# Round 0 of an RWKV-6 + MLP kernel: two tiles transposed from padded copies instead of turned by products, masks built together, and a new order of work

## The chip, the core and the metric

One core of one Trainium2 chip. The engines are PE (TensorE: matmuls and weight loads), DVE (VectorE), ACT (ScalarE), POOL (GpSimd), and SP, whose queue issues nearly all DMAs. The metric is the device time of one execution in microseconds (us), lower is better.

## What is computed

A linear-attention block with a decayed state (RWKV-6), and behind it a normalised two-layer MLP with a residual. Everything is float32.

```python
B, H, S, D = 4, 8, 768, 48            # r, k, v, w: (B, H, S, D); u: (H, D)
state = np.zeros((B, H, D, D))
for t in range(S):
    cur = einsum('bhd,bhe->bhde', u[None] * k[t], v[t])
    y[t] = einsum('bhd,bhde->bhe', r[t], state + cur)
    state = w[t][..., None] * state + einsum('bhd,bhe->bhde', k[t], v[t])
x = y.transpose(0, 2, 1, 3).reshape(B, S, 384)
xn = (x - mean) / sqrt(var + 1e-6) * g_ln
out = x + relu(xn @ w_ch1) @ w_ch2    # w_ch1: (384, 1536), w_ch2: (1536, 384)
```

## The kernel before, in words

**Rounds and tiles.** The work is cut into 8 rounds (4 batches, two halves of 384 steps). A round has 3 tiles of 128 steps, and a tile is two groups of 64 rows. For the attention part, r, k and w are loaded as nat_r, nat_k and nat_w (192 KB a tile; in a row lie 2 heads x 4 steps x 48 values). They are turned so that the head dimension lies on the partitions: two heads of a pair stand at partitions 0 to 47 and 64 to 111. Between them is a gap of 16, so a source whose heads are padded from 48 to 64 values can be turned in one piece.

**Round 0 differs from the others.** It has two parts: tile 0 alone, and tiles 1 and 2 together (`parts_of_round`, line 513), so that tile 0 can run ahead. Its r, k and w are turned by `by_head` (line 746): two products with the identity for each row group and step, straight from the unpadded loads. `turn` (751) does this for k and r of one tile into kr_ps (PE), and two copies out of PSUM ("keep") bring it to kr. `whole_row` (827) does it for w into one of the "a" tiles, and a copy brings it to low. The other rounds work on padded tiles pad_k and pad_r, which DVE, POOL and ACT write (`inner`, 596), and `turn` transposes these with one PE.transpose for each row group and step.

**Behind the turning** there is a ladder of 6 levels for each part: `quads` (952) does products of k and r on PE into an "a" tile; `keep` (1008) copies them, masked by that level's mask, into A on DVE; `grow` (984) multiplies kr by the products of w of that level (DVE); `totals` (921) makes the next level's products of w (low, then tot; DVE or POOL). Level l+1 of quads needs level l of grow. `own_terms` (855) does r times u (ru) and the products with k (own), masked by the diagonal. Then come `turn_k`, `states`, `outputs`, the normalisation, and the MLP's `first_product` and second product.

**Masks.** Five level masks, the diagonal and a row-group mask (own) are built by POOL at the start: `build_mask` (470) does, for each level, a memset, two affine selects on a 128 x 64 byte strip of "wide" and two copies of 64 x 32 bytes to mask0..mask4. `build_own_mask` (487) is needed from round 1 on only.

**Weights.** The MLP's weights come as 24 raw loads of 384 KB into 4 buffers, and each is converted by some three instructions of ACT, DVE or POOL (`convert`); a buffer is free when its conversions are done.

**What sets the order.** Every job is announced with `plan.add` (engines with costs, keys read and written) and gets a number in that order. `Plan.ORDER` (74) is a list written out by hand: job number, plus 10000 or 20000 where the second or third allowed engine does it. Each engine works its jobs strictly in that order. `Plan.order` (223) walks the list once; it also places "idle" matmuls on zeros wherever by its own costs PE would wait over 0.35 us (line 2011). A job on POOL that is marked as sharing the port first waits for the DVE jobs listed just before it. Neither the conversions nor rounds 1 to 7 are touched by the change other than through the order.

The heads of the queues, as they follow from the list before:

- PE: k, r of tile 0; w of tile 0; quads level 0 of tile 0; own of tile 0; k, r of tile 2; quads 1 of tile 0; k, r of tile 1; w of tile 2; quads 0 of tiles 1+2; w of tile 1; quads 2 of tile 0; own of tiles 1+2; quads 3, 4, 5 of tile 0; quads 1 of tiles 1+2.
- DVE: A zeroed; second copy of kr tile 0; r times u; keep 0; totals 0; grow 0; own terms; a conversion; grow 1; totals; keep 1; keep 0 of tiles 1+2; ...
- POOL: masks 3, 0, diagonal, masks 2, 4, 1, totals 1, r times u of tiles 1+2, totals, own mask.
- SP: r, w of tile 0, k of tile 2, u_t twice, r 2, k 1, r 1, raw2, w 1, w 2, g, raw4, raw1, v, u_bc, raw0, raw5, w of round 1, raw3, vx.

Of the kernel before, what the change touches and what calls it, by code (L numbers as in the profile page):

```python
# [62 lines left out]
class Plan:  # L63
# [11 lines left out]
        15, 4, 3, 19, 20, 12, 8, 14, 2, 250, 11, 10, 16, 13, 9, 252, 249, 251, 17, 10021, 28, 31, 33, 29, 95,  # L75
        260, 247, 18, 262, 22, 32, 34, 30, 10096, 35, 257, 97, 261, 259, 258, 10023, 24, 25, 36, 248, 255, 256,
        98, 10269, 272, 253, 274, 0, 254, 263, 107, 91, 93, 92, 94, 59, 5, 87, 37, 38, 88, 109, 89, 90, 270,
        111, 433, 103, 60, 39, 439, 10264, 10026, 271, 40, 265, 42, 41, 273, 43, 44, 46, 110, 108, 7, 10266, 45,
        51, 50, 99, 47, 55, 275, 276, 105, 113, 10027, 127, 49, 48, 52, 53, 10054, 61, 100, 106, 129, 6, 277,
        56, 112, 10101, 62, 65, 66, 63, 123, 434, 436, 1, 440, 441, 435, 114, 104, 278, 10064, 102, 279, 115,  # L80
        119, 438, 10267, 139, 69, 67, 57, 70, 58, 68, 71, 128, 130, 373, 280, 281, 282, 72, 444, 73, 125, 74,
        75, 283, 126, 375, 76, 120, 77, 124, 284, 285, 287, 78, 131, 79, 121, 122, 141, 437, 10080, 443, 81, 85,
        83, 288, 142, 286, 303, 10268, 10134, 10084, 82, 86, 293, 301, 10289, 10294, 442, 116, 295, 296, 193,
        305, 304, 143, 300, 292, 297, 298, 291, 290, 10445, 10118, 10117, 306, 309, 225, 227, 223, 302, 446,
        299, 194, 307, 308, 310, 132, 449, 133, 377, 228, 312, 311, 313, 314, 224, 144, 315, 135, 316, 237, 140,
        136, 238, 226, 137, 229, 230, 10450, 239, 235, 233, 10317, 10318, 319, 320, 321, 322, 323, 324, 325,
        447, 240, 138, 10326, 181, 236, 234, 327, 329, 331, 195, 451, 231, 448, 328, 332, 145, 458, 10330, 151,
        10452, 10453, 232, 183, 196, 182, 335, 184, 388, 345, 346, 336, 455, 457, 454, 456, 169, 153, 459, 163,
        627, 337, 338, 374, 185, 460, 461, 152, 462, 469, 389, 10146, 10154, 376, 197, 147, 349, 463, 333, 474,
        473, 475, 350, 465, 392, 464, 378, 149, 466, 341, 468, 467, 393, 155, 156, 148, 482, 150, 476, 347, 403,  # L90
        198, 624, 157, 159, 164, 170, 348, 158, 379, 470, 355, 404, 483, 485, 477, 167, 173, 186, 480, 621, 626,
        187, 625, 342, 334, 161, 339, 241, 245, 486, 10471, 10472, 407, 171, 382, 160, 10380, 10162, 390, 172,
        242, 479, 478, 351, 246, 481, 487, 484, 488, 165, 188, 391, 628, 629, 622, 623, 632, 489, 385, 340, 166,
        352, 175, 177, 176, 179, 191, 490, 343, 243, 353, 491, 178, 10168, 217, 418, 244, 634, 189, 356, 631,
        635, 180, 174, 496, 405, 493, 354, 219, 367, 357, 344, 633, 190, 494, 492, 500, 505, 502, 501, 495, 220,
        506, 394, 630, 192, 637, 406, 368, 638, 636, 497, 211, 381, 213, 499, 218, 10386, 507, 199, 498, 200,
        643, 203, 221, 408, 358, 508, 205, 10639, 10640, 513, 509, 644, 514, 10222, 510, 400, 201, 214, 212,
        202, 420, 215, 204, 645, 10216, 664, 663, 662, 206, 397, 515, 516, 207, 422, 503, 409, 209, 412, 208,
        210, 395, 641, 421, 642, 398, 504, 511, 512, 387, 812, 399, 362, 396, 363, 10401, 661, 402, 520, 364,
        646, 815, 365, 366, 415, 647, 657, 10658, 517, 518, 383, 659, 384, 648, 521, 809, 10416, 10410, 10413,  # L100
        359, 411, 813, 560, 650, 649, 10522, 10519, 523, 524, 525, 526, 654, 419, 360, 655, 527, 528, 529,
        10530, 656, 531, 532, 533, 541, 361, 542, 534, 543, 537, 538, 535, 423, 539, 424, 369, 651, 652, 430,
        653, 816, 665, 570, 417, 814, 565, 370, 667, 544, 536, 668, 540, 666, 670, 10431, 10660, 571, 561, 566,
        811, 810, 545, 671, 555, 414, 572, 427, 428, 562, 573, 425, 371, 563, 10819, 669, 672, 673, 546, 674,
        567, 574, 568, 547, 564, 432, 817, 556, 548, 426, 429, 550, 580, 575, 676, 551, 10821, 569, 549, 557,
        552, 558, 675, 820, 823, 822, 576, 818, 677, 585, 577, 586, 553, 554, 587, 559, 679, 581, 588, 600, 590,
        733, 589, 582, 601, 602, 578, 579, 753, 595, 825, 826, 678, 684, 680, 691, 827, 583, 831, 685, 603, 584,
        687, 686, 596, 695, 696, 697, 688, 10828, 833, 10830, 10824, 698, 832, 829, 682, 693, 604, 597, 694,
        591, 598, 683, 689, 699, 599, 690, 681, 700, 605, 1000, 743, 849, 1003, 850, 997, 692, 836, 701, 705,
        592, 838, 837, 842, 702, 971, 1002, 703, 593, 606, 704, 594, 706, 844, 839, 841, 843, 708, 10707, 607,  # L110
        834, 608, 748, 851, 1005, 1001, 999, 998, 1004, 852, 11007, 709, 10710, 711, 713, 712, 714, 715, 1009,
        716, 717, 835, 720, 10719, 10718, 840, 609, 610, 845, 1008, 721, 1010, 722, 729, 725, 846, 858, 726,
        11006, 730, 723, 727, 724, 728, 731, 1013, 732, 615, 611, 616, 758, 853, 738, 855, 883, 854, 1011, 856,
        612, 744, 734, 11014, 859, 10847, 11012, 1019, 857, 861, 1015, 745, 735, 736, 737, 617, 11016, 863, 862,
        746, 749, 864, 747, 750, 613, 754, 618, 751, 755, 752, 1018, 860, 1021, 1017, 1020, 614, 865, 866, 867,
        1024, 1090, 1087, 1037, 1093, 884, 768, 773, 848, 1040, 1039, 778, 756, 1026, 1025, 871, 769, 619, 868,
        1038, 739, 757, 770, 876, 870, 877, 878, 740, 771, 873, 772, 874, 1094, 788, 1088, 872, 875, 869, 741,
        1027, 889, 783, 890, 1029, 742, 1028, 885, 1091, 886, 1030, 1032, 1031, 784, 759, 1022, 1089, 789, 785,
        786, 760, 887, 790, 1023, 879, 888, 1092, 1041, 1095, 761, 774, 762, 1098, 1096, 1097, 1101, 791, 779,
        775, 880, 776, 780, 777, 936, 1042, 1043, 372, 763, 781, 793, 1100, 792, 764, 782, 881, 891, 765, 892,  # L120
        11099, 1045, 1044, 1103, 1104, 1109, 1110, 1046, 893, 894, 1105, 11106, 11107, 1111, 11108, 766, 794,
        767, 895, 787, 882, 896, 795, 798, 897, 10898, 899, 1047, 1049, 1114, 1102, 11033, 901, 900, 902, 903,
# [212 lines left out]
def kernel(  # L335
# [12 lines left out]
    nc = tc.nc  # L348
# [121 lines left out]
    def build_mask(lev):  # L470
# [8 lines left out]
        for i in range(2):  # L479
            rows = ds(C * i, C)  # L480
            POOL.tensor_copy(out=masks[lev][rows], in_=wide[lev][rows, ds(C // 2 * i, C // 2)])
# [1571 lines left out]
```

## Time and profile before

| what | value |
|---|---|
| median of 3 runs | 499.63 us (496.48 to 505.93) |
| the profiled execution, its own time | 494.83 us |
| its span, first to last instruction | 492.8 us |
| mean granted TensorE clock | 0.996 |
| PE busy | 479.1 us (97%), 26.55 us of it "idle" filler matmuls |
| DVE, ACT, POOL busy | 351.2, 256.6, 114.6 us |
| DMA | 57.39 MB, mean 116 GB/s |

How to read it: nearly all instructions bear line 46, that of the wrapper through which the kernel issues them, so one goes by tile names. "kr_ps<-ident,nat_r" is a product of k or r, "a<-ident,nat_w" one of w, "a<-kr" a quad, "kr_ps<-ident,pad_r" a transpose of the later rounds, "mask<-wide" a copy of a finished mask. In a timeline row stand start, length, engine, operation, output<-input, shape and count, and in brackets what the engine waited for before it. "issue" is time in which the engine waited for nothing that the profile shows. A span on POOL is rough.

### The profile page before, as it was taken

Reading aid. Unit: us, or ns where it says so; the run is one execution under the profiler, and the core shown is the slowest. Engines: PE = TensorE matmul, PEld = TensorE weight load, DVE = VectorE, ACT = ScalarE, POOL = GpSimd, SP = SyncE. Lnnn points to the kernel's source line nnn. Section 1 sums busy time; section 2 is a strip of 40 time slices with the busy share of each in tenths; the row PEclk is TensorE's granted clock in tenths of the full one; section 3 lists DMA queues with packets and bytes.
Section 4 is the critical chain, followed back from the end, with each engine's and each line's share of the span. In section 5 each row is a group of like instructions: output and inputs, shape, how many; then the busy total and the mean of one; then the engine's idle time right before and its main releaser. Section 6 shows DMA issues by size and latency. Waiting matters only on the chain.

```text
span 492.8 us, 18752 instructions
## 1 busy us (share of the span) xinstructions
PE 479.1 (97%) x8215; PEld 406.6 (83%) x8215; DVE 351.2 (71%) x694; ACT 256.6 (52%) x585; POOL 114.6 (23%) x127
## 2 busy tenths in 40 slices
PE   8799999999999999999999999998999999999996
PEld 6667887667986779966888776788999999999996
DVE  6689899997975994877684796978667355345334
ACT  3569988964485217625635517476643243232231
POOL 8433404441311510131820660002300000000000
PEclk9989999999999999999999999999999999999999
DMA  7677388248946327347338605230331221223301
GB/s 205 181 216 189 106 193 241 61 121 210 255 99 175 57 66 180 98 121 165 122 102 198 188 4 100 67 76 5 96 98 50 76 86 43 85 64 93 117 0 48
DMA packets 102113, 57.39 MB, mean 116 GB/s; under 512 B 58256, under 2 KB 98704, under 8 KB 102032
## 3 DMA queue, kind: packets, MB, share of 16 engines
q1 hardware_dynamic: 101760, 56.01, 43.3%
q8 instruction: 64, 1.05, 0.9%
q10 hardware_dynamic: 272, 0.20, 0.1%
q14 instruction: 17, 0.14, 0.1%
HBM read 45.81 MB, written 8.01 MB: 109 GB/s over the span
## 4 chain that ended last, share of the span: by engine, by line
PE 85%; ACT 6%; DVE 3%; issue 2%; POOL 2%; DMA 1%; SPq 0%; DVEq 0%; POOLq 0%; ACTq 0%
PE h_ps L46 30%; PE a L46 25%; PE o L46 16%; PE o_2P L46 3%; PE kr_ps L46 3%; PE idle L46 3%; PE o_2D L46 2%; PE xT_ps L46 2%; PE kn_ps L46 1%; ACT rest L46 1%; DMA d<-w1d 1%; POOL tot L46 1%; ACT rx L46 1%; ACT held L46 1%; DVE x L46 1%
## 5 line engine op out<-in xcount | busy, mean ns | idle before, releaser
L46 PE MATMUL o<-ffn,h 128*128 128x384 f32 x288 | 101.6, 495 | 0.0
L46 ACT ACTIVATE h_ps<-h_ps 128x384 f32<-128x384 f32 x84 | 39.5, 475 | 71.8 <-PE h_ps L46 66.7
L46 PEld LDWEIGHTS o<-ffn,h 128*128 128x128 f32 x288 | 52.1, 189 | 29.4
L46 DVE TENSOR_TENSOR kr<-kr,tot 112x1536 f32<-112x1536 f32 (+2 forms) x36 | 60.2, 1673 | 13.3 <-PE a L46 13.1
L46 DVE SCALAR_TENSOR_TENSOR hL<-h_ps,hH 128x384 fp32r<-128x384 f32 x48 | 26.5, 555 | 57.9 <-ACT hH L46 57.3
L46 PEld LDWEIGHTS a<-kr 48*60 48x60 f32 (+5 forms) x3264 | 42.8, 122 | 10.1 <-issue 5.3
L46 PE MATMUL h_ps<-xd,d 128*128 128x384 f32 x204 | 49.3, 350 | 0.4 <-DMA d<-w1d 0.4
L46 PE MATMUL a<-kr 48*60 48x32 f32 (+5 forms) x3264 | 47.2, 209 | 1.3 <-issue 0.8
L46 PE MATMUL h_ps<-xhl,wl 128*128 128x384 f32 x180 | 44.5, 354 | 1.2 <-issue 1.2
L46 ACT ACTIVATE hH<-h_ps 128x384 fp32r<-128x384 f32 x48 | 23.2, 491 | 41.0 <-PE h_ps L46 40.9
L46 PE MATMUL h_ps<-xhl,wh 128*128 128x384 f32 x180 | 41.4, 338 | 0.0
L46 PEld LDWEIGHTS h_ps<-xd,d 128*128 128x128 f32 x204 | 35.7, 188 | 2.1 <-issue 0.5
L46 ACT COPY kr<-kr_ps 112x512 f32<-112x512 f32 x47 | 26.2, 587 | 20.5 <-PE kr_ps L46 20.3
L46 ACT ACTIVATE h<-h_ps 128x384 f32<-128x384 f32 (+2 forms) x60 | 24.9, 425 | 20.5 <-PE h_ps L46 20.0
L46 PEld LDWEIGHTS h_ps<-xhl,wl 128*128 128x128 f32 x180 | 31.5, 188 | 3.5 <-issue 1.5
L46 PE MATMUL a<-xkr,hH 128*128 128x384 f32 x96 | 32.4, 337 | 0.0
L46 PEld LDWEIGHTS h_ps<-xhl,wh 128*128 128x128 f32 x180 | 32.4, 188 | 0.0
L46 DVE COPY_PREDICATED A<-mask,a 128x768 f32<-128x768 int8 (+2 forms) x31 | 28.2, 910 | 4.4 <-PE a L46 4.2
L46 PE MATMUL idle<-nought 128*128 128x128 f32 (+2 forms) x86 | 26.6, 417 | 1.0 <-DVE eps L46 1.0
L46 DVE SCALAR_TENSOR_TENSOR hD<-hH,hL 128x384 fp32r<-128x384 f32 x48 | 26.2, 555 | 0.9
L46 PE MATMUL h_ps<-xf,w 128*128 128x128 f32 (+1 forms) x144 | 25.9, 332 | 0.0
L46 PE MATMUL a<-sx,rx 48*64 48x48 f32 x384 | 23.7, 218 | 1.8 <-issue 1.3
(195 smaller groups left out, 1098.0 us busy)
## 6 DMA issues: line engine op xcount, KB each, us to landing
d<-w1d SPq DMA_DIRECT2D x84, 192.0 KB, 3.0
raw<-in_moe_w_ch_dram SPq DMA_DIRECT2D x24, 384.0 KB, 4.0
nat_r<-in_r_dram SPq DMA_DIRECT2D x24, 192.0 KB, 3.8
nat_w<-in_w_dram SPq DMA_DIRECT2D x24, 192.0 KB, 4.1
v<-in_v_dram SPq DMA_DIRECT2D x24, 192.0 KB, 4.5
nat_k<-in_k_dram SPq DMA_DIRECT2D x23, 192.0 KB, 3.8
w1d<-w1diff SPq DMA_DIRECT2D x12, 192.0 KB, 3.6
out_dram<-x SPq DMA_DIRECT2D x4, 576.0 KB, 3.7
```

The lines of the kernel that those rows point to most:

```text
L46: ins = self.tc.keep_in_program_order(f(*args, **kw))
```

## The change

Three things. (1) Tiles 1 and 2 of round 0 are no longer turned by `by_head`: two copies pad k and r into the tiles pad_k and pad_r, a third pads w into a borrowed "x" tile (pad_w, its gap zeroed by a memset), each on any of ACT, DVE and POOL, and PE transposes them as in the other rounds. Tile 0 stays as it was. (2) The masks of levels 1 to 4 become one job behind mask 0's: one memset for all five strips, the ten selects as before, and two copies for four levels together. (3) The order list is new in its whole length, and the plan's instruction counts for the products are doubled.

```diff
-    masks = {lev: const.tile([P, C // 2], I8, name=f"mask{lev}") for lev in range(NLEV - 1)}
+    masks = const.tile([P, NLEV - 1, C // 2], I8, name="masks")
...
-    def build_mask(lev):
-        n = 1 << lev
-        m = wide[lev].rearrange("p (q n) -> p q n", n=n)
-        POOL.memset(m, 1.0)
-        for base, sign in ((0, 1), (n - 1, -1)):
-            POOL.affine_select(
-                out=m, in_=m, compare_op=ALU.is_ge, fill=0.0, base=base,
-                pattern=[[-2 * n * sign, C // n], [0, n]], channel_multiplier=sign,
-            )
+    def build_masks(levels):
+        if 0 in levels:
+            POOL.memset(wide, 1.0)
+        for lev in levels:
+            n = 1 << lev
+            m = wide[:, lev].rearrange("p (q n) -> p q n", n=n)
+            for base, sign in ((0, 1), (n - 1, -1)):
+                POOL.affine_select(
+                    out=m, in_=m, compare_op=ALU.is_ge, fill=0.0, base=base,
+                    pattern=[[-2 * n * sign, C // n], [0, n]], channel_multiplier=sign,
+                )
+        some = slice(levels[0], levels[-1] + 1)
         for i in range(2):
             rows = ds(C * i, C)
-            POOL.tensor_copy(out=masks[lev][rows], in_=wide[lev][rows, ds(C // 2 * i, C // 2)])
+            POOL.tensor_copy(out=masks[rows, some], in_=wide[rows, some, ds(C // 2 * i, C // 2)])
...
+    def unpadded(part):
+        return part[0] == part[1] == 0
...
-                        if rnd == 0:
+                        if unpadded(part):
                             by_head(to[:, n, s], f"nat_{nm}0", c, s, rows)
                             continue
                         PE.transpose(
...
     def whole_row(part):
         rnd, c0, nc = part
+        n = nc * Q * 2 * D
+        w_pad = f"pad_w{c0}"
+
+        def roomy():
+            t = tile_("x", w_pad, [P, TT, H, D]).rearrange("p c h d -> p (c h d)")
+            return t[:, 0 : nc * Q * 2 * HP].rearrange("p (s c j d) -> p s c j d", s=Q, c=nc, j=2)
+
+        def copy(e, nm):
+            src = natural(nm, part).rearrange("p s b d -> p b s d")
+            if nm == "w":
+                to = roomy().rearrange("p s c j d -> p (c j) s d")[..., 0:D]
+            else:
+                to = padded(nm, part).rearrange("p s b d -> p b s d")
+            (ACT.copy if e == "ACT" else BY[e].tensor_copy)(out=to, in_=src)
+
+        if not unpadded(part):
+            plan.add("POOL", 0.35, lambda: POOL.memset(roomy()[..., D:], 0.0), ...)
+            for nm in "wkr":
+                plan.add(("ACT", "DVE", "POOL"), ..., lambda e, nm=nm: copy(e, nm), ...)
...
                 for s in range(Q):
                     for i in range(2):
-                        by_head(t[:, i, s], "nat_w0", c, s, ds(C * i, C))
+                        rows = ds(C * i, C)
+                        if unpadded(part):
+                            by_head(t[:, i, s], "nat_w0", c, s, rows)
+                            continue
+                        PE.transpose(
+                            t[:, i, s], roomy()[rows, s, c - c0].rearrange("p j d -> p (j d)")[:, 0:PD],
+                            ident[rows, rows],
+                        )
...
-            for lev in range(NLEV - 1):
+            for levels, cost_ in (((0,), 1.7), (range(1, NLEV - 1), 3.5)):
                 plan.add(
-                    "POOL", 1.5, lambda lev=lev: build_mask(lev), r=["wide"], w=[("mask", lev)],
-                    pri=lev - 40, port=False,
+                    "POOL", cost_, lambda levels=levels: build_masks(levels), r=["wide"] + [("mask", 0)] * (0 not in levels),
+                    w=[("mask", lev) for lev in levels], pri=levels[0] - 40, port=False,
                 )
...
     ORDER = [
-        15, 4, 3, 19, 20, 12, 8, 14, 2, 250, 11, 10, 16, 13, 9, 252, 249, 251, 17, 10021, 28, 31, 33, 29, 95,
+        2, 14, 9, 7, 8, 12, 10015, 10019, 20, 4, 3, 16, 17, 248, 10, 11, 247, 249, 10018, 25, 28, 26, 246, 13,
+        250, 10252, 30, 29, 253, 258, 261, 262, 259, 263, 245, 0, 244, 10260, 21, 104, 31, 27, 1, 20251, 256,
```

Three mask jobs fall away and four jobs come (250 the memset, 251, 252 and 253 the copies of w, k and r), so the later jobs' numbers are moved. The heads of the queues after:

- PE: w of tile 0; k, r of tile 0; quads 0 of tile 0; own of tile 0; k, r of tile 1; k, r of tile 2; quads 1 of tile 0; w of tile 2; w of tile 1; quads 0 of tiles 1+2; quads 2 of tile 0; own of tiles 1+2; quads 3, 4, 5 of tile 0; quads 1 of tiles 1+2.
- DVE: A zeroed; copy of low tile 0; totals 1 of tile 0; second copy of kr tile 0; r times u; **copy k**; keep 0; grow 0; a copy of kr tile 1; totals; own terms; keep 1; r times u of tiles 1+2; totals; grow 1; keep 0 of tiles 1+2; keep 2; grow 2; a sign conversion; own terms of tiles 1+2; keep 3; grow 3; grow 0 of tiles 1+2; grow 4; ...
- POOL: own mask; diagonal; mask 0; totals 0 of tile 0; masks 1 to 4; memset of pad_w; g_top; **copy w**; totals 0 of tiles 1+2; ...
- ACT: first copy of kr tile 0; **copy r**; three copies of kr tiles 2, 1; two copies of low; conversions.
- SP: w, r of tile 0, r 1, u_t twice, k 2, r 2, k 1, w 2, g, w 1, raw4, raw5, r of round 1, raw0, raw1, w of round 1, raw2, v, raw3, raw10, raw8, vx.

## The prediction

> **What bounds the kernel now.** I read the page first, then busy time by stage, then the chain of waits up to 60 us, then the timelines of PE, DVE and POOL up to 27 us.
>
> The page and the busy time by stage (columns: stretch, its length, busy time and instructions of each engine, granted clock, DMA share, GB/s):
>
> ```profile
> span 492.8 us, 18752 instructions
> ```
> ```profile
> 5.00:17.00 12.00, 8.92 (x375) 7.36 (x365) 5.94 (x12) 4.72 (x9) 8.59 (x22) 1.00 0.87 245
> 17.00:25.00 8.00, 7.49 (x238) 5.67 (x230) 7.07 (x11) 5.00 (x11) 3.07 (x8) 1.00 0.56 145
> 25.00:37.00 12.00, 11.25 (x329) 8.57 (x328) 10.08 (x21) 8.57 (x24) 3.62 (x6) 0.86 0.77 220
> 37.00:50.00 13.00, 12.87 (x332) 10.19 (x329) 12.96 (x35) 12.47 (x32) 4.03 (x5) 1.00 0.67 179
> ...
> 62.00:75.00 13.00, 13.00 (x265) 10.73 (x265) 12.66 (x24) 10.89 (x24) 1.72 (x1) 1.00 0.82 197
> ```
>
> From 62 us on PE is full. Before that it only looks full: of PE's 26.55 us of filler ("idle") matmuls, 22.1 lie before 50 us and 0.9 between 50 and 62. So up to 25 us round 0 runs on a chain of single steps (DVE is busy for 13.0 of the 20 us from 5 on, ACT for 9.7); from 37 to 50 us DVE (12.96 of 13 us) and ACT (12.47) are the bound; from then on it is PE. Everything that the change names lies in the first stretch. What it gains there reaches the end only as an earlier start of the same later work.
>
> The chain of waits (start, length, what) and PE's timeline at the same place:
>
> ```profile
> 8.58 0.80 PE kr_ps L46 x49
> 9.38 0.61 issue
> ...
> 10.86 0.96 PE kr_ps L46 x58
> ...
> 13.27 2.18 issue
> ...
> 16.40 1.10 PE a L46 x64
> ...
> 17.52 1.31 DVE A L46
> ...
> 18.87 1.78 PE a L46 x78
> ```
> ```profile
> 12.81 0.46 PE L46 MATMUL a<-ident,nat_w 64*64 64x64 f32 x14
> ...
> 15.45 0.53 PE L46 MATMUL a<-ident,nat_w 64*48 64x64 f32 x18 [2.18 <-issue]
> ...
> 61.22 0.44 PE L46 MATMUL kr_ps<-ident,pad_r 64*112 64x64 f32 x8
> ```
>
> The reader is to see that the products of tiles 1 and 2 (kr_ps, and "a" from nat_w) are on the chain, and that two stalls of 0.61 and 2.18 us fall in the middle of one tile's products, whose data had arrived. Between the two stalls PE ran 127 matmuls and 126 weight loads (busy time from 9.39 to 13.30); from the second to the next "issue" stall at 26.5 it ran 382 and 383. That is 253 and 765, three times 255: the stalls come every so many instructions, so it is the supply of instructions that ran out, at a DMA share of 0.97.
>
> **Products against transposes.** In the trace a product of this kind is two matmuls and two weight loads; a transpose (round 1's, from pad_r and pad_k) is one of each. A tile's k and r are 32 products, its w 16: for tiles 1 and 2 that is 2 x (128 + 64) = 384 instructions. As transposes they are 16 and 8: 2 x (32 + 16) = 96. A tile's k and r take 0.96 us as products (4.28 to 5.24) and 0.59 as transposes (61.22 to 61.81): 2 x 0.37 saved. For w, half of that, 0.37. With the stalls of 2.79 us gone, PE has 3.9 us less to do between 8.4 and 16. How much of it the path keeps depends on what is late next, which the walk below finds: the copy of w.
>
> **The copies.** Each pads 768 elements a row for two tiles. r on ACT: the 576-element copy takes 0.66, so 0.87; ACT is idle then (3.88 us before its copy at 10.48), cost nothing; without that cover 0.87. k on DVE: no such row; between 0.57 (a 384-element tensor-scalar) and 1.0 (0.75 for 576 with two inputs, scaled); I take 0.8, for it has one input but as many elements. w on POOL: the 576-element pad copy took 0.66, 0.99 and 2.22 (least, median, most), so 0.88 to 2.96, and I take 1.3.
> The spread is what POOL suffers beside DVE: two selects of one mask took 0.65 alone and 1.37 beside DVE's memset. The Trainium skill says so too: SBUF — State Buffer, in its section on two physically separate sides, makes the port pair of the two an exclusive lock, so that POOL waits out a whole DVE instruction; by it the copy would be 1.3 plus one 1.26 us multiply, 2.6, still inside these ends.
>
> **The masks.** Five sets of memset, two selects, two copies become 1 + 10 + 4 instructions, but the new list puts the row-group mask (2.1 us in the trace, from 21.24) and the diagonal (0.57) ahead of mask 0. From 2.18, where POOL starts masks now: 2.1 + 0.57 + one mask of 2.1 (1.44 to 2.18) = 6.95. Behind it the product of w pairs, 0.61: 7.56. DVE now has the next such product (0.28) third in its queue, and behind that its kr copy (0.69) and r times u (0.69): they end at 8.5 and 9.2. Before, the kr copy started at 5.53 and the first level-0 products (a<-kr) at 6.31; they now start at 8.55, 2.2 later. The first own terms start at 9.25, not 7.88.
> Masks 1 to 4: eight selects at 0.53 (mean of 1.06 a pair; 0.33 to 0.69) are 4.25, two larger copies 1.0 (0.6 to 1.6): POOL is at 12.8. A memset 0.4 and g 0.2: 13.4. Copy of w 1.3: 14.7.
>
> **The walk.** DVE: copy k to 10.0, masked copy 10.5, multiply 0.69 to 11.2. PE: k and r of tiles 1 and 2 from 10.0 to 11.2 (before: to 11.81); level 1 at 11.25 (before 10.16). w of tiles 1 and 2: 14.75 to 15.4 (before 12.81 to 15.98, and 17.24 to 17.9). Level 0 of tiles 1 and 2, 1.1 us, to 16.5. Level 2 of tile 0 starts there, if DVE's level-1 multiply is done: 11.2 + copy 0.69 + product 0.28 + masked copy 0.72 + masked copy 0.5 + times u 1.26 + 0.28 + multiply 0.69 = 15.6, yes. So 16.5 against 18.87: 2.4 earlier. Then DVE's steps, 1.29 + 0.43 + 0.69, give level 3 at 18.95 (20.99 before); 0.35 + 1.31 + 0.43 + 0.68 give level 4 at 21.7 (23.25); 1.26 + 0.68 give level 5 at 23.5 (25.03). That is 1.5 earlier; the new list puts the own terms and a sign conversion in, which eat the rest of the 2.4. From there both lists have the same chain.
> SP's queue. Its loads take 0.6 to 0.7 us each to issue. Both w loads of tiles 1 and 2 now go ahead of the first weight load (raw), which is issued at about 8 and not at 6.04; it lands some 4 us later, and ACT, busy with copies out of PSUM to 15.4, doesn't miss it. The fifth raw waits for one of four buffers, until ACT's first conversion ends (15.4 + 3 x 0.57 = 17.1; SP waits now as well, 6.0 us from 11.5). Behind it in the queue are the load of v (issued at 10.10 now) and, three raws later, its swap vx (20.48 now): v lands at 17.2 + 4.5 = 21.7, vx at about 26, and their readers start at 30.7 and 33.5 now. So not late, with 7 us or more of slack. u_bc moves 12 places down the queue (issued at 10.6 now); its product with k starts at 50.4 now.
> Counted in the two lists, ACT has 81 jobs ahead of round 0's last output product before and 82 after, DVE 58 and 57: about the same work. So the full stretch from 37 us starts 1.5 us earlier and is no longer. Without that cover the two copies' 0.87 + 0.8 would be paid there, and the change costs 0.2.
> The rest of the list, rounds 1 to 7, is new as well. No row prices that. PE is full there, so nothing is to be won but its idle time: 1.21 and 1.32 us of "issue" at 256 and 338, and 3.5 of filler after 100 us, 6.0 in all. I take 0, with ends of -6 and +6 (as much again lost).
> The granted clock was 0.63 and 0.87 in 27.3 to 34.1, 1.7 us of clock lost, mostly on filler; it may fall elsewhere, so 1.7 either way.
>
> **Sum.** -1.5 - 0 = -1.5 us, against the profiled execution's 494.83 us (span 492.8): 493.3. The three runs' median is 499.63, 4.8 above that execution, so 498.1 in such runs.
>
> **Rivals.** A, the stall stays. If PE's 2.18 us is not supply of instructions, level 0 of tiles 1 and 2 starts up to 2.2 later and level 2 at 18.7; the gain is 0.2 and ACT's full stretch eats it: 499.6. For: DMA was at 0.97 there and may delay anything; against: 253 and 765. The Trainium skill, Runtime: NRT & Kernel Launch, Instruction fetch mechanics, says that instructions come in blocks of 256, which the trace bears out, but that this is mostly hidden; by it fewer instructions win nothing and 499.6 is the time. The 2.18 us speak against the second half.
> B, POOL is late (slower). Its place is the copy of w, behind all masks. It decides from the point where that copy ends after 16.2 (14.7 + the 1.5 gained). At POOL's upper ends, 7.56 + 5.5 + 1.6 + 0.6 + 2.96 = 18.2; level 2 then starts 1.1 later than now, and the 0.9 that the new list puts between the levels comes on top: +2.0, 501.6. For: POOL's selects beside DVE; against: the medians.
> C, the rest of the list gains its 6.0: 498.1 - 6.0 = 492.1. For: PE's idle time there is known; against: it lies behind waits of 1 us in different rounds.
> D, the rest loses as much: 504.1. For: nothing fixes those waits' number; against: PE had 0 filler between 160 and 300 us.
>
> **Numbers.** Forecast 0.40, A 0.19, B 0.20, C 0.13, D 0.08. The likeliest alone: 496 to 499.5 (ends of copy k, of the masks, and the clock). Range for 8 in 10: 492.0 to 503.0, C's value at one end, B with the clock's 1.7 at the other, D out. About 2%, 10 us, is what a measurement of this kernel tells from no change (the three runs go from 496.48 to 505.93). 489.6 is only reached by C and the clock and luck, 0.05; 509.6 by D and the same, 0.05; within 2%: 0.90.
>
> **What would show it.** kr_ps and w of tiles 1 and 2 at a quarter of the instructions and no stall of over 1 us before 18 us; first level-0 products at about 8.5; copy of w ending at 14 to 16; level 5 of tile 0 at about 23.5; DVE's full stretch beginning at about 35.5; PE's filler before 50 us smaller by less than 4. Wrong, if the first level-0 products start before 7, if the copy of w ends after 17, or if the span differs by more than 3 us from a cause after 62 us.

## The result, and the profile after

The changed kernel takes 496.74 us (median of 20 runs, 493.45 to 499.39); the kernel before, on the same chip, 500.39 (20 runs, 496.48 to 509.21). The ratio is 0.9933, with an interval of 0.9908 to 0.9958: 0.7% faster. A second measurement, beside runs of before of its own, gave 494.97 against 498.55, a ratio of 0.9944 (0.9912 to 0.9975). The ratios here, and the clock lost in the table below, leave out executions that lie more than 1.5% above the fastest of their kernel (the profiled ones of e4 and e10 are such); the medians are over all.

The two profiled executions stand the other way round: 498.02 us of its own time after (span 496.2) against 494.83 before. The profiled execution of before was faster than all 20 of the runs just named (lowest 496.48). So the gain can't be read as a difference of these two pages. What can be read from them is where each step stands.

The page of the changed kernel (span; then busy time and instructions of each engine):

```profile
span 496.2 us, 18437 instructions
PE 482.6 (97%) x8071; PEld 406.9 (82%) x8071; DVE 355.8 (72%) x708; ACT 253.7 (51%) x579; POOL 102.0 (21%) x113
```

Its busy time by stage (stretch, length, the five engines, granted clock, DMA share, GB/s), to be held against the stretches of before:

```profile
5.00:17.00 12.00, 12.00 (x321) 8.90 (x314) 8.34 (x16) 5.13 (x10) 8.01 (x19) 1.00 0.86 255
17.00:25.00 8.00, 7.01 (x153) 5.36 (x146) 6.66 (x10) 5.61 (x12) 1.73 (x3) 0.79 0.80 223
25.00:37.00 12.00, 11.17 (x368) 8.67 (x366) 10.63 (x24) 10.32 (x30) 4.55 (x5) 1.00 0.64 175
37.00:50.00 13.00, 12.41 (x288) 9.63 (x284) 11.50 (x31) 11.20 (x29) 3.99 (x6) 1.00 0.73 198
```

Between 5 and 17 us PE has no wait left that the profile shows: 12.00 of 12 us, where it had 8.92 (part of it is filler). DVE is no longer full between 37 and 50 us (11.50 of 13, before 12.96). But in 17 to 25 us the granted clock is 0.79, where it was 1.00.

PE's timeline of the changed kernel:

```profile
4.08 1.13 PE L46 MATMUL a<-ident,nat_w 64*64 64x64 f32 x32 [0.59 <-DMA nat_w<-in_w_dram]
5.14 1.65 PE L46 MATMUL idle<-nought 128*128 128x384 f32 x2
6.72 1.13 PE L46 MATMUL kr_ps<-ident,nat_r 64*64 64x64 f32 x32
7.61 1.09 PE L46 MATMUL kr_ps<-ident,nat_k 64*48 64x64 f32 x32
...
10.03 0.66 PE L46 MATMUL a<-kr 48*63 48x32 f32 x32
...
12.25 0.39 PE L46 MATMUL kr_ps<-ident,pad_k 64*112 64x64 f32 x8
...
14.27 0.78 PE L46 MATMUL a<-ident,pad_w 64*112 64x64 f32 x16
...
15.61 1.54 PE L46 MATMUL a<-kr 48*63 48x32 f32 x91
18.14 0.30 PE L46 MATMUL a<-kr 48*60 48x32 f32 x5 [0.99 <-issue]
...
25.32 1.49 PE L46 MATMUL a<-kr 48*32 48x32 f32 x96
```

The reader is to see four things. The first level-0 products start at 10.03. Tiles 1 and 2 are turned in a quarter of the instructions: 32 for k and r in 1.1 us (11.53 to 12.64), 16 for w in 0.78. The stalls inside that turning are gone, but one of 0.99 us has come at 17.15, with 27 of level 2's 32 products issued and 5 to go. And level 5 of tile 0 starts at 25.32, not before the 25.03 of the kernel before, whose PE timeline has it here:

```profile
25.03 1.48 PE L46 MATMUL a<-kr 48*32 48x32 f32 x92
```

POOL's timeline (row-group mask, mask 0's selects, the low product, the copies of masks 1 to 4, the copy of w):

```profile
2.96 0.80 POOL L46 TENSOR_SCALAR mask_and<-wide 64x64 int32<-64x64 int8 x2
...
4.81 1.38 POOL L46 TENSOR_SCALAR_AFFINE_SELECT wide<-wide 128x64 int8<-128x64 int8 x2
...
6.79 0.61 POOL L46 TENSOR_TENSOR low<-low 112x256 f32<-112x256 f32 x1
...
11.24 0.99 POOL L46 COPY masks<-wide 64x128 int8<-64x128 int8 x2
...
13.39 0.82 POOL L46 COPY pad_w<-nat_w 128x768 f32<-128x768 f32 x1
```

So path and median disagree: the path of round 0 isn't shorter in this profile, yet the median is lower. The experiments look for what else the change took away.

**The theories.** T1: PE's stalls are its instruction supply; the change helps by needing fewer instructions, and what a stall costs is the stall and the slow clock behind it. T2: the padded turning is a shorter path and that is the gain; the stalls are something else (DMA load, data). T3: the new order, not the turning, carries the gain. T4: the masks do.

Each run lists its mean granted clock. "Clock lost" below is (1 - that clock) x its time, median over the executions that the ratio counts. It is an estimate of what the clock cost, for it takes all work to go at PE's pace. "Stall" is PE's "issue" wait nearest to its 698th instruction, in the profiled execution.

| kernel | median (range, runs; counted in the ratio where fewer) us | ratio to before | clock lost us | stall us | clock in 17 to 25 us |
|---|---|---|---|---|---|
| before, on three chips | 500.80 (33; 25), 498.51 (35; 28), 498.55 (35; 22) | 1 | 7.1, 6.0, 5.7 | 2.18 | 1.00 |
| changed, again | 494.97 (492.16 to 496.68, 12) | 0.9944 [0.9912, 0.9975] | 1.0 | 1.32 | 0.79 |
| e1 turning alone | 498.44 (491.88 to 506.06, 12; 6) | 0.9907 [0.9872, 0.9942] | 1.0 | none | 1.00 |
| e2 masks alone | 501.49 (497.04 to 506.63, 12; 11) | 1.0019 [0.9986, 1.0052] | 7.0 | 3.81 | 0.50 |
| e3 all but the turning | 503.87 (501.59 to 509.95, 10; 9) | 1.0065 [1.0024, 1.0107] | 7.5 | 2.51 | 0.50 |
| e4 new head, old order behind | 498.32 (491.66 to 502.78, 12; 7) | 0.9907 [0.9866, 0.9947] | 2.5 | 1.24 | 0.57 |
| e5 old head, new order behind | 500.58 (496.69 to 501.94, 12) | 1.0035 [1.0003, 1.0067] | 6.5 | 2.38 | 0.54 |
| e6 row-group mask late | 496.60 (493.11 to 498.50, 12) | 0.9957 [0.9928, 0.9986] | 3.5 | 1.72 | 1.00 |
| e7 k and r first | 496.50 (494.50 to 498.94, 12) | 0.9974 [0.9941, 1.0008] | 3.0 | none | 0.50 |
| e8 more instructions ahead | 500.50 (499.86 to 501.71, 12) | 1.0040 [1.0016, 1.0064] | 0.5 | none | 1.00 |
| e9 e6's head, old order behind | 495.13 (489.45 to 502.59, 12; 11) | 0.9914 [0.9872, 0.9956] | 1.5 | 1.53 | 0.79 |
| e10 round 0 rebuilt | 495.14 (491.39 to 504.72, 12; 7) | 0.9905 [0.9866, 0.9944] | 2.5 | 1.83 | 0.79 |
| e11 loads late | 499.15 (497.21 to 503.90, 12) | 1.0016 [0.9983, 1.0048] | 3.5 | none | 1.00 |

The runs of e1 to e4 share one chip and its runs of before (500.80), e5 to e8 another (498.51), and the last four a third (498.55).

### The profile page after: what moved, and what is told of

Read it like the earlier page. It is cut to its first block, busy times and chain, and to the rows that moved or that the text cites. A ratio compares the mean times of both kernels' runs of the same rounds, so it can differ in the third digit from the quotient of the medians.

```text
span 496.2 us, 18437 instructions
## 1 busy us (share of the span) xinstructions
PE 482.6 (97%) x8071; PEld 406.9 (82%) x8071; DVE 355.8 (72%) x708; ACT 253.7 (51%) x579; POOL 102.0 (21%) x113
## 3 DMA queue, kind: packets, MB, share of 16 engines
q8 instruction: 63, 1.03, 0.9%
## 4 chain that ended last, share of the span: by engine, by line
PE 78%; DVE 6%; ACT 5%; DMA 3%; SPq 3%; issue 2%; POOL 2%; DVEq 0%; POOLq 0%
PE h_ps L46 27%; PE a L46 22%; PE o L46 15%; PE o_2P L46 3%; SPq L46 3%; PE kr_ps L46 3%; PE idle L46 2%; PE o_2D L46 2%; PE xT_ps L46 2%; DVE A L46 2%; DMA nat_r<-in_r_dram 1%; DMA d<-w1d 1%; ACT rx L46 1%; PE kn_ps L46 1%; DVE kr L46 1%
## 5 line engine op out<-in xcount | busy, mean ns | idle before, releaser
L46 DVE TENSOR_TENSOR kr<-kr,tot 112x1536 f32<-112x1536 f32 (+2 forms) x36 | 57.6, 1600 | 11.3 <-PE a L46 11.1
L46 ACT ACTIVATE hH<-h_ps 128x384 fp32r<-128x384 f32 x48 | 23.5, 489 | 47.6 <-PE h_ps L46 47.5
L46 DVE COPY_PREDICATED A<-masks,a 128x768 f32<-128x768 int8 (+2 forms) x31 | 28.0, 904 | 3.4 <-PE a L46 2.8
```

The lines of the kernel that those rows point to most:

```text
L46: ins = self.tc.keep_in_program_order(f(*args, **kw))
```

## The experiments

**e1: the turning alone.** Before's masks and order; only tiles 1 and 2 padded and transposed, the four new jobs put in.

```diff
-                        if rnd == 0:
+                        if unpadded(part):
...
-        15, 4, 3, 19, 20, 12, 8, 14, 2, 250, 11, 10, 16, 13, 9, 252, 249, 251, 17, 10021, 28, 31, ...
+        15, 4, 3, 19, 20, 12, 8, 14, 2, 250, 11, 10, 16, 13, 9, 252, 249, 251, 256, 17, 10021, 28, 10255, 31, ...
```

> The kernel before with the turning alone: tiles 1 and 2 padded by three copies (r on ACT, k on DVE, w on POOL) and transposed; the old masks, and the old order with the four new jobs put in. Theory 1 (the gain comes from round 0's turning, by PE's instructions and the stalls that they cause): no stall of over 1 us in the products of tiles 1 and 2, level 2 of tile 0 some 2 us before 18.87, and 1 to 3 us less in all (ratio 0.994 to 0.998). Theory 2 (the gain comes from the new order of rounds 1 to 7): 0.999 to 1.002.

0.9907: by this ratio the turning alone gives the whole gain; whether it gives more than the whole change isn't shown, for the intervals overlap (0.9872 to 0.9942, and 0.9908 to 0.9958). The ratio counts 6 of e1's 12 runs; by the medians over all it is 0.5% (498.44 against 500.80), and the whole change 0.7%. Level 2 of tile 0 starts at 17.99, 0.9 us before 18.87 and not some 2. In its profile PE has no "issue" stall before 37 us. The one that comes then is long. Its timeline has it here:

```profile
39.71 0.64 PE L46 MATMUL a<-kr 48*48 48x32 f32 x36 [2.06 <-issue]
```

**e2: the masks alone.** Before with the levels 1 to 4 built in one job.

```diff
-            for lev in range(NLEV - 1):
+            for levels, cost_ in (((0,), 1.7), (range(1, NLEV - 1), 3.5)):
```

> The kernel before with the masks alone built in two jobs, on the old order. Both theories: POOL's masks are done about 0.5 us sooner, nobody on the path waits for them, ratio 0.998 to 1.002. A third, that POOL's masks hold up the masked copies of round 0: 0.995 to 0.998.

1.0019, no difference that can be told from none, so T4 falls. Its profile shows best what a stall does. PE's timeline, and the next stretches:

```profile
17.64 0.87 PE L46 MATMUL a<-ident,nat_w 64*48 64x64 f32 x18 [3.81 <-issue]
```
```profile
17.00:25.00 8.00, 7.36 (x206) 6.65 (x210) 3.04 (x4) 4.05 (x9) 0.48 (x1) 0.50 0.29 82
25.00:37.00 12.00, 11.52 (x235) 7.93 (x232) 9.32 (x16) 5.98 (x16) 5.02 (x11) 0.78 0.70 208
```

The stall stands at the same 18 products of w as in before. Behind it the granted clock is 0.50 for the whole of 17 to 25 us.

**e3: all but the turning.** The changed kernel's order and masks, with tiles 1 and 2 turned by products again.

```diff
-                        if unpadded(part):
+                        if rnd == 0:
...
-        if not unpadded(part):
-            plan.add("POOL", 0.35, lambda: POOL.memset(roomy()[..., D:], 0.0), ...)
-            for nm in "wkr":
-                plan.add(("ACT", "DVE", "POOL"), ..., lambda e, nm=nm: copy(e, nm), ...)
```

> The changed kernel with the turning undone: all three tiles by products, no padding copies; new masks and new order stay. Theory 1: the 288 instructions come back, PE stalls of 2 us or more return before 18 us, and the time is that of before or worse, 1.000 to 1.006. Theory 2: the gain stays, 0.992 to 0.996.

1.0065: without the turning the new order is a loss. T3 falls. The stall is back, in the middle of the products of w (PE's timeline, and the stretch behind it):

```profile
17.20 1.54 PE L46 MATMUL a<-ident,nat_w 64*48 64x64 f32 x45 [2.51 <-issue]
```
```profile
17.00:25.00 8.00, 7.15 (x238) 6.93 (x239) 3.40 (x5) 5.82 (x12) 1.83 (x3) 0.50 0.43 89
```

**e4: the new head, before's order behind it.** The changed kernel with the first 234 entries of its list, the rest in before's order.

```diff
-    ORDER = [...]                      # the changed kernel's 2015 entries
+    ORDER = [...]                      # its first 234, then before's entries that are left
```

> The changed kernel's code with its order up to round 0's last output product (the first 234 entries of the list), and from there on the old order. Theory 1: the whole gain, 0.992 to 0.996. Theory 2: none, 0.999 to 1.003.

0.9907, as e1. So the old and the new head are worth the same once the turning is in, and the new order of the later rounds adds nothing to the new head.

**e5: the old head, the new order behind it.**

```diff
-    ORDER = [...]                      # before's 2015 entries
+    ORDER = [...]                      # its first 229, then the changed kernel's entries that are left
```

> The code of before, the first 229 entries of before's order (round 0 up to its states), and behind them the order of the changed kernel. If the order of rounds 1 to 7 is worth nothing, as the forecast took it, the ratio to before is 1.000, between 0.997 and 1.003, and the stalls of 0.6 and 2.2 us at PE's instructions 443 and 696 are there as before. The rival, that the new order behind round 0 carries part of the gain, gives 0.995 or less with the stalls still there.

1.0035 (1.0003 to 1.0067): the new order of the later rounds costs some 1.7 us (0.35% of 498.5). The stalls are where they were (0.86 and 2.38 us). The second comparison of the same thing agrees in sign but doesn't decide by itself: the changed kernel at 0.9944 against e9, before's order behind nearly the same head, at 0.9914, on one chip, where the medians are the same (494.97 and 495.13). So the cost is shown without the turning only. The forecast had 0 here.

**e6: the row-group mask behind the copy of w.** One entry is moved.

```diff
-        2, 14, 9, 7, 8, 12, 10015, 10019, 20, 4, 3, ..., 0, 244, 10260, 21, 104, 31, 27, 1, 20251, 256,
+        2, 14, 9, 8, 12, 10015, 10019, 20, 4, 3, ..., 0, 244, 10260, 21, 104, 31, 27, 1, 20251, 7, 256,
```

> The changed kernel with the row-group mask built behind the copy of w and no longer ahead of mask 0. The forecast's working (POOL's masks set the first level-0 products) gives mask 0 done at 4.9 in place of 6.7 and the first level-0 products about 2 us earlier, at 8.0. The theory after the result: the load of r stands second in the queue and its products behind filler on a cold PE, so kr_ps comes last, at 8.7, whatever POOL does; the first level-0 products stay at 10.0 (9.7 to 10.2), the copy of w ends 1.5 us earlier, and the ratio is that of the changed kernel, 0.993, within 0.002.

POOL's masks came as expected: mask 0 was done at 5.1 and the low product at 6.6; the copy of w was done at 13.6, 0.6 us earlier than in the changed kernel and not 1.5. The first level-0 products start at 8.99 in this profile, and at 10.33 in that of e9, which has the same head. The difference between the two is not POOL's: here the products of k take 0.65 us, there 1.09, because PE gets its full clock at 7.22 us here and at 10.01 there (see below, under the first level-0 products). PE's timeline of e6:

```profile
6.55 0.97 PE L46 MATMUL kr_ps<-ident,nat_r 64*64 64x64 f32 x32
7.34 0.65 PE L46 MATMUL kr_ps<-ident,nat_k 64*48 64x64 f32 x32
...
8.99 0.66 PE L46 MATMUL a<-kr 48*63 48x32 f32 x32
...
18.24 0.30 PE L46 MATMUL a<-kr 48*60 48x32 f32 x5 [1.72 <-issue]
```

So kr_ps comes last, as the theory after the result had it; my bounds of 9.7 to 10.2 were too narrow. What is gained at 8.99 is lost at the stall: the block of instructions doesn't come earlier, so the wait grows from 0.99 to 1.72, and the 5 last products start at 18.24 (18.14 in the changed kernel). The ratio, 0.9957 (0.9928 to 0.9986), is a little over the 0.991 to 0.995 that was expected, and not to be told from it.

**e7: k and r of tile 0 first.** e6, and r loaded and k and r turned ahead of w.

```diff
-        2, 14, 9, 8, 12, 10015, 10019, 20, 4, 3, 16, 17, 248, 10, 11, 247, 249, 10018, 25, 28, 26, ...
+        4, 3, 2, 9, 12, 8, 16, 17, 10018, 14, 248, 10, 11, 25, 10015, 10019, 28, 26, 247, 249, ...
```

> The changed kernel with three things moved in round 0: r of tile 0 loaded ahead of w, its k and r turned ahead of its w on PE, and the row-group mask built behind the copy of w. If the load order and PE's order set the first level-0 products, they start at 7.4 to 7.8 in place of 10.0, level 2 of tile 0 starts at about 16, or stays at 17 or later if the instruction supply holds it, and the ratio falls from 0.993 to 0.989. If those 2.5 us are hidden behind later work, the ratio stays at 0.993.

The first level-0 products start at 7.22, so the load order and PE's order did set them. But nothing came of it (0.9974, dearer than either case that was expected): POOL's low product now waits 3.62 us for DVE, POOL falls behind, and the copy of w ends at 16.1. POOL late was rival B of the prediction; here another order made it so. POOL's timeline, PE's, and the stretch behind:

```profile
14.26 1.84 POOL L46 COPY pad_w<-nat_w 128x768 f32<-128x768 f32 x1
```
```profile
16.15 0.66 PE L46 MATMUL a<-ident,pad_w 64*112 64x64 f32 x16 [2.34 <-POOL wide L46]
```
```profile
17.00:25.00 8.00, 8.00 (x198) 6.65 (x199) 4.08 (x7) 7.42 (x16) 2.65 (x6) 0.50 0.52 122
```

Here PE stood still for 2.34 us for data, not for instructions, and the clock behind it is 0.50 just the same. So a standstill doesn't have to be one for instructions to be followed by half clock.

**e8: 128 more instructions ahead.** Meant to move the boundaries of the supply against the work.

```diff
+    small = [68]
+
     def idle(n, home):
         t = banks.tile([P, 512], F32, tag=f"b{home}", name="idle")
+        if small:
+            for _ in range(small.pop()):
+                PE.matmul(t[0:48, 0:32], zeros[:, 0:48], nought.broadcast_to([P, 32]), start=True, stop=True)
+            return
```

> The changed kernel, with its first four filler products replaced by 68 small ones, so that 128 more instructions stand ahead of PE's work and nothing else changes. If PE stalls wherever its next 256 instructions have not come (at 442, 698, 1208 and 1720 in all kernels so far), the stall inside the first quads of tiles 1 and 2 and level 2 (349 matmuls and 349 weight loads, 0.99 us in the changed kernel) is no longer there; a stall comes 64 matmuls earlier or 64 later in the work instead: at the end of the own terms of tiles 1 and 2, at about 20 us and again at 349 or 413 real instructions pairs counted with the small ones, 0.5 to 2 us long. If the stall belongs to the data of level 2, it stays at level 2 of tile 0. The time: 0.993 of before, within 0.004.

It doesn't answer its question. Each small product is two matmuls and two weight loads, not one of each, so the shift was 132 of both, 264 instructions: one whole block, after which the boundaries lie where they lay. And they are slow:

```profile
0.99 11.09 PE L46 MATMUL idle<-nought 128*48 128x32 f32 x136 [0.99 <-DVE eps L46]
```

They end at 12.0, so round 0 starts 7.9 us later. Still it shows something: no "issue" stall before 33 us, since round 0's loads have landed by then (DMA share 0.46 in 17 to 25 us, 0.80 in the changed kernel); a clock loss of 0.5 us, the least of all kernels, and 12 runs within 1.9 us of each other. And a start 7.9 us later costs only some 5 us by the ratios (1.0040 against 0.9933 and 0.9944).

**e9: e6's head, before's order behind it**, made as e4 from e6's list.

> The changed kernel's first 234 entries with the row-group mask behind the copy of w, and before's order for the rest. The runs so far put the gain at -0.9% for the turning and +0.3% for the new order of the later rounds; if these add up, this comes to 0.990 of before and 0.997 of the changed kernel. If the new order of the later rounds is needed for the new head, it comes out at 0.993 or more.

0.9914, on one chip with the changed kernel at 0.9944. It lies between the two expectations, and the intervals overlap.

**e10: round 0 rebuilt.** k and r first, all masks in one go, the low product on DVE, its copy on ACT, before's order from entry 234 on.

```diff
-        2, 14, 9, 7, 8, 12, 10015, 10019, 20, 4, 3, 16, 17, 248, 10, 11, 247, 249, 10018, 25, 28, 26, ...
+        4, 3, 2, 9, 12, 8, 13, 16, 17, 10018, 14, 15, 248, 10, 11, 25, 19, 28, 26, 247, 249, 246, 250, ...
```

> Round 0 rebuilt from what the runs showed: k and r of tile 0 loaded and turned ahead of w, masks 0 to 4 in one go on POOL with the low product on DVE, the copy of w straight behind them, the row-group mask behind that; before's order from entry 234 on. First level-0 products at 7.3, copy of w done at 12, no wait of PE over 1.7 us before 25 us and so no half clock in 17 to 25; level 5 of tile 0 at about 23 in place of 25.3. If the start of round 0 counts, 0.987 of before; if only the missing stall counts, 0.990.

0.9905, the lowest ratio, but not to be told from e1, e4 and e9, and by the median no better than the changed kernel (495.14 against 494.97). The first level-0 products start at 7.13, but POOL stands idle for 3.46 us and its copy of w ends at 13.97 and not at 12; PE then waits 1.83 us for instructions at the same place as ever, the clock in 17 to 25 us is 0.79, and level 5 of tile 0 starts at 25.92 and not at about 23. No version here beats the changed kernel in the median.

**e11: the weight loads held back.** The first weight load of SP's queue waits for a one-element write by ACT, so that the DMA engines are idle when the block of instructions is due. All else is the changed kernel.

```diff
+            to = tile_("raw", raw_, [P, WC, 2], I32).rearrange("p n two -> p (n two)")
+            if i == 4:
+                ACT.copy(out=to[0:1, 0:1].bitcast(F32), in_=eps[0:1, 0:1])
             SP.dma_start(
-                out=tile_("raw", raw_, [P, WC, 2], I32).rearrange("p n two -> p (n two)"),
+                out=to,
```

> The changed kernel, in which the first weight load waits for a one-element write of ACT behind its copies of kr, so that all loads from the first weights on start at about 13.5 in place of 8.0 and the DMA engines are nearly idle from 11.5 to 13.5. If the length of the instruction stall is set by the load on the DMA engines, the block of instructions that arrives at 15.5 in the changed kernel arrives at 13 to 14.5, and the stall of 0.99 us at 17.15 is gone or under 0.3. If the arrival has a time of its own, the stall stays at 0.8 or more. The time is not the point: the weights come 5 us later, and ACT's conversions may cost up to 5 us, 0.993 to 1.003.

The trace has a DMA queue named "q8 instruction", whose packets are 16 KB (1.03 MB in 63 packets in the changed kernel's page). In the changed kernel one of them starts at 15.77, in e11 at 13.62. PE passes its 443rd instruction at 12.8 there and 13.2 here, so the block comes 3.0 us after that with the DMA engines at 0.92, and 0.45 us after it with the engines idle. The stall is gone. The DMA share stands in the last but one column (the changed kernel's stretch, then two of e11), then comes PE's timeline of e11:

```profile
12.00:13.00 1.00, 1.00 (x55) 0.93 (x50) 0.84 (x4) 0.33 (x1) 0.54 (x2) 1.00 0.92 318
```
```profile
11.00:12.00 1.00, 1.00 (x42) 0.81 (x36) 0.89 (x2) 0.00 (x0) 0.84 (x4) 1.00 0.00 0
12.00:13.00 1.00, 1.00 (x37) 0.93 (x40) 0.79 (x2) 0.00 (x0) 0.21 (x1) 1.00 0.00 0
```
```profile
15.96 1.56 PE L46 MATMUL a<-kr 48*63 48x32 f32 x96
...
26.26 0.56 PE L46 MATMUL a<-kr 48*48 48x32 f32 x32 [4.42 <-DVE kr L46]
```

All 96 quads run in one piece, where the changed kernel broke off after 91. The late weights cost more than that: a sign conversion in DVE's queue waits for them, and PE with it, 4.42 us. That is about the price: 499.15 us against the changed kernel's 494.97 on the same chip.

## Why the prediction came out as it did, step by step

The number was near (498.1 forecast, 496.74 measured, and 494.97 in the second measurement), but by luck: two steps failed, the 1.5 us on the path didn't come, and the largest term, the clock, was missing from the sum.

**Instruction supply: right.** Counted as matmuls plus weight loads from the start, PE's "issue" stalls up to 45 us stand at these instructions:

| instructions | stalls (us) |
|---|---|
| 443 | before 0.61, e2 0.32, e5 0.86 |
| 696 to 698 | before 2.18, e2 3.81, e5 2.38, e3 2.51, changed 0.99 and 1.32, e4 1.24, e6 1.72, e9 1.53, e10 1.83 |
| 1461 | before 0.75 |
| 1717 to 1720 | e1 2.06, changed 0.17 twice, e4 0.30, e6 0.17, e9 0.17, e10 0.39, e11 0.44 |
| 1974 | e3 0.33 |

What PE does there differs (k of tile 2, w of tile 2, level 2 of tile 0, level 4); the count doesn't. With PE's semaphore instructions counted as well it is 193 + 256 n exactly, in all 23 stalls: 449, 705, 1473, 1729, 1985. Three more "issue" waits aren't of this kind: the 0.52 us of e4 and e7 and the 0.53 of e8, at 1216, 1221 and 1480, come at the first product with v, where the changed kernel waits 0.83 us for ACT, and the packet of their block had started 4.2 to 5.4 us before. In the others PE goes on 2.2 to 2.9 us after the start of the block's packet (2.3 to 2.5 in all ten at 698). That is also why e1 and e7 have no stall there: their packets start at 14.72 and 16.70, and PE gets to 698 only 3.5 us later, at 18.2 and 20.1. With e11, T1 holds for the stalls: blocks of 256 instructions, fetched through the DMA engines that carry the loads. Rival A, that the stall is something else, falls. The Trainium skill, Runtime: NRT & Kernel Launch, Instruction fetch mechanics, says that instructions come in 16 KiB blocks of 256, which the packets and the counts bear out, and that the cost of a boundary is mostly hidden. Of eleven kernels that passed instruction 698 with the loads under way, nine paid 0.99 to 3.81 us there, all but e1 and e7; with the loads late or over, e11 and e8 paid nothing.

**"With the stalls gone": failed.** The step took 2.79 us of stall for gone. The prediction had the count, 253 and 765, but did not ask what stands at instruction 698 in the new order. It is the level-0 quads of tiles 1 and 2 and level 2 of tile 0, the next step of the same path. So the stall moved behind the turning and shrank to 0.99; it didn't go.

**The copies and the masks: right.** r 0.83 (0.87 forecast), k 0.55 (0.8), w 0.82 (1.3); low product done at 7.40 (7.56), masks 1 to 4 at 12.2 (12.8), copy of w at 14.2 (14.7). Rival B didn't come, for the copy of w ended before its 16.2; in e7 it ended at 16.1, and most of the gain was gone. The Trainium skill, SBUF — State Buffer, in its section on two physically separate sides, would have had the copy of w wait out a DVE instruction, 2.6 us by the prediction's estimate. In the changed kernel DVE ran only masked copies out of PSUM beside it, and it took 0.82, so that trace doesn't decide; in e7 a DVE product with two inputs (r times u, 1.25 us from 14.17) lay over it and it took 1.84, so there the trace agrees.

**The first level-0 products: failed.** Forecast 8.55, measured 10.03. The working followed POOL's masks. But in the new list w of tile 0 is loaded and turned first, so the products of r stand behind filler of 1.65 us, and PE's products ran more slowly: 1.13 us for 32, where before took 0.69. PE's timeline of before:

```profile
0.99 3.36 PE L46 MATMUL idle<-nought 128*128 128x384 f32 x6 [0.99 <-DVE eps L46]
4.28 0.69 PE L46 MATMUL kr_ps<-ident,nat_r 64*64 64x64 f32 x32
4.77 0.66 PE L46 MATMUL kr_ps<-ident,nat_k 64*48 64x64 f32 x32
...
6.31 0.66 PE L46 MATMUL a<-kr 48*63 48x32 f32 x32
```

The slow products are the clock. The trace's record of it begins when the full clock is first granted, at 4.30 us in before and at 8.91 in the changed kernel; what lies ahead of it reads 1.00 only because nothing is recorded. The six filler matmuls at the start take 3.36 us, as six take at a clock of 0.50 (3.35 in e4 at 21.51), and 1.78 at full clock. In all 14 profiles these products are slow ahead of the first grant and fast behind it. So of the 1.5 us that the forecast missed some 0.8 are slow products (1.98 us for k and r against 1.15), and 0.5 is filler, which ends at 10.1, when DVE's copy of kr had ended at 9.49. kr_ps was done at 8.7, when mask 0 and the low product had long been ready. e6 and e9 (mask early: 8.99 and 10.33) against e7 and e10 (k and r first: 7.22 and 7.13) show which of the two it was. The 2.2 us that I charged to the row-group mask was the load order's and PE's.

**Level 2 to 5.** Level 2 of tile 0 was forecast for 16.5 and starts inside the row at 15.61, behind 64 quads, at about 16.7 (15.68 + 64/91 of 1.47); then come the stall and the clock of 0.50 between 20 and 22 us. Level 3 starts at 20.27 (18.95 forecast), level 4 at 23.55 (21.7), level 5 at 25.32 (23.5). The gain of 1.5 us on the path isn't there; e11 without the stall has level 3 at 19.55. And the time that PE no longer spends on turning went into filler: 23.02 us of it before 50 us, where before had 22.14 and the forecast said less.

**The later order, forecast 0 between -6 and +6:** it costs 0.35% without the turning (e5), 1.7 us, inside the bounds; with the turning no cost is shown.

**The clock: the missing term.** I took before's median, 4.8 us above its profiled execution, as a constant on both sides and the clock as 1.7 us either way. The gain came out of this 4.8. Before loses 5.7 to 7.1 us of clock in the median, the changed kernel 1.0 in both measurements. The four kernels with a standstill of PE of over 2.3 us between 13 and 18 us (e2, e3, e5, and e7 for data) all have a granted clock of 0.50 to 0.54 in 17 to 25 us; the three with none of over 0.8 us there (e1, e8, e11) all have 1.00. Over the runs of before, time and clock lost go together (correlation 0.49 to 0.80). Without the clock's share nothing is gained: time less clock lost is 491.7 to 492.3 in the median for before, and 495.6 and 493.8 for the changed kernel. The executions with a clock of 0.995 or more say the same without that estimate: 10 of before's have a median of 494.8 us, 25 of the changed kernel's 495.3. What the change does is to have more such executions: 25 of 32, against 10 of 75. T2, a shorter path, is thus not what lowers the median. The turning's 0.9% and the later order's 0.35% come to -0.6% by the ratios, against -0.7 and -0.6 measured; by the medians over all they come to about nothing (-0.5 and +0.4), so that this sum proves little.

**How a standstill costs the clock.** The traces show more than lengths. In the 14 traces, the half-clock spells that don't run into the end last 3.41, 6.83, 10.24 or 13.65 us, so the clock changes on a grid with a step of 3.41 us. Up to 45 us, each step at full clock in which PE was busy for 0.55 of it or less was followed by half clock (8 of 8); of those between 0.57 and 0.78, 5 of 15; of those above, none. So it counts where on the grid a standstill falls. Before's 2.18 us lie across a border, at 14.54: PE is busy for 0.63 and 0.73 of the two steps, and the clock stays full; its 0.75 us at 26.5 lie in one step (0.78), and half clock follows. e6's 1.72 us are split as well (0.72 and 0.77), the changed kernel's 0.99 are not (0.71). e11's 4.42 us leave 0.57 and 0.14, and cost one step of half clock. The grid lies differently in each execution, for the first grant comes between 3.96 and 14.30 us. That fits single executions of before that scatter by 3%, and a change that shortens a standstill of over 2 us to about 1; that the grid makes the scatter is not shown, for only one execution of each measurement was traced.

What stays open: what decides between 0.57 and 0.78, and when the full clock comes back: in the changed kernel after one step, in e5 and e7 after three, with PE busy throughout. And no run has the later order's cost with the turning in and the heads alike.

## What to carry to other kernels

Before a stall is counted as saved, count the instructions up to it: if it stands at the same count in every version, fewer instructions only move it along the program, and the thing to look up is what will stand at that count afterwards. A bunch of tiny matmuls just where the loads are heaviest is a bad place for it (1 to 3.8 us here), since the instructions come through the same DMA engines. And when single executions scatter by 3%, look at each run's granted clock before the path: a change can lower the median by shortening a standstill of PE and leave the path as long as it was.

## What the runs showed of the hardware that was not expected

- The granted clock changes on a grid of 3.41 us, and half clock followed each step in which PE was busy for 0.55 or less, for data (e7) as for instructions (e2, e3, e5). Behind standstills of 2.3 to 3.8 us it lasted 10.2 to 13.7 us, behind e11's 4.42 us 3.4. The Trainium skill, TensorE: Matmul & The Clock Gate, HAM oscillation, gives as its rule no idle gaps above some 3.4 us; here 2.34 us were enough, so the measurement is the stricter of the two.
- The time of a block of instructions depends on the load: 3.0 us from the boundary before it to its packet at a DMA share of 0.92 (2.6 to 5.3 us in the profiles of all eleven kernels with the loads under way), 0.45 us with the DMA engines idle. From its packet to PE's next instruction it took another 2.4 us in the changed kernel (15.77 to 18.14).
- PE runs at half clock at the start, until a first grant of full clock at 3.96 to 14.30 us, and the profile's clock reads 1.00 for that time: 32 products of 64 x 64 took 1.13 us ahead of the grant and 0.69 behind it (e1 and before, both from 4.28, with the grant at 6.86 and 4.30).
- A product shows as two matmuls and two weight loads, a transpose as one of each. The matmuls of a product over 128 rows with 32 columns took 82 ns each (e8: 11.09 us for 136), those of the 48-row quads with 32 columns 16 ns (e11: 1.56 us for 96).
